# A new order of all steps in an attention and two-layer MoE kernel on one Trainium2 core

## The chip, the cores and the metric

The kernel runs on one core of a Trainium2 chip. The metric is device time in microseconds (us) of one execution. Five engines matter: TensorE (PE) with its weight loads (PEld), VectorE (DVE), ScalarE (ACT), GpSimd (POOL), and SyncE (SP), whose queue issues every DMA transfer here. Each engine works through its own queue strictly in the order in which the program issues; semaphores make it wait for others.

## The reference

For 4 batches and 8 heads, 768 time steps and head width 40, a gated linear attention with a stabilised state, then two feed-forward layers over 3072 tokens of width 320:

```python
for t in range(S):                                   # attention, per batch and head
    m_new = max(f[t] + m, i[t])
    C = exp(f[t] + m - m_new) * C + exp(i[t] - m_new) * outer(v[t], k[t])
    n = exp(f[t] + m - m_new) * n + exp(i[t] - m_new) * k[t]
    m = m_new
    y[t] = sigmoid(o[t]) * (C @ q[t]) / max(abs(n @ q[t]), 1)
h = x @ w_in                                         # layer 1: 320 -> 1024
solu = h * softmax(h)
x2 = ((solu - mean(solu)) / sqrt(var(solu) + 1e-6) * g_ln) @ w_out
h2 = max(x2 @ w1, x2 @ w2, x2 @ w3)                  # layer 2: 320 -> 768
out = h2 @ w2_out
```

## The kernel before, in words

The attention is done in chunks of 128 time steps: 24 tiles t, four batches of six chunks, all eight heads at once. A tile's 128 tokens then pass through layer 1, and each pair g of two tiles through layer 2. Products run in a 32-bit float form whose operands are split into a high and a low part (helper `split`, L274 and L276: ACT copies the high part, another engine subtracts it), so one product is two or three passes.

The program is a set of Python generators. Each does the work of one kind for one tile, pair or weight piece, and hands over at each `yield`; what stands between two yields is a step. The string `ORDER` names one step after another, and that is the order in which all instructions are issued, and so each engine's queue. In it `A0*2` is two steps of process A0, and a number behind `~` puts as many small products that nothing reads in front of the step's own, to keep PE active. The order is written out as it stands; nothing is chosen at run time.

```python
        for token in ORDER.split():
            token, _, z = token.partition("~")
            spare[0] = int(z or 0)
            name, _, n = token.partition("*")
            for _ in range(int(n or 1)):
                next(procs[name])
```

The processes, and what their steps issue:

- G: gates. Scans on DVE make the row maxima and decays; they are turned by PE, and rows_m, rows_g and rows_d go to DRAM to be read back spread over partitions.
- L*key*: loads of weight pieces, 640 KB each, 20 in all: in0 and in1 (two each), out0 to out3, nine m*, last0 to last2. D0 to D19 decode them (L249 to L299): two steps of ACT, two of DVE, an addition on GpSimd (L261), then the split or the scaling of the weights.
- Q*t*: loads q and k. From tile 6 on they are split (L274, L276), both parts go to DRAM (qks, L348) and come back stacked three times over 120 partitions as kst and qst (L355, six transfers of 160 KB), which have one buffer each. W*t*: the decay mask Wm, a 512 KB load (L385), a mask on GpSimd (L367), exponentials on ACT (L396). V*t*: values and keys. I*t*: gb, a 192 KB load of decays, and either its product with q (qg, L441, tiles under 6) or products pi of PE (L452). T*t*: the state (L464 to L492). S*t*.0 and S*t*.1: score products ps (L423) and their masking Pr (L426).
- Y*t*: output products py (L501 and on), copies, then a store of the denominators nd (L516) and of y (L517), three small DVE operations on nd (L519 to L521) and a store of rn (L523). X*t*: loads xr (L536 to L538) and nq (L540, spread from rn), products with the output gate and nq (L542, L544), and the split into xh and xl. O*k*: the output gate's sigmoid on ACT.
- A*t*: layer 1. Two products ph (L566), maxima (L569), exponentials (L573), u (L578), squares (L581), the scaling of u (L591), its transposes pu (L599), splits, the product px (L615), the transposes pq (L627) and the split of x2.
- U*g*: nine products pe of a pair (L650), in two PSUM buffers. P*g*: their maximum (ACT copies the first of three, L662; DVE takes the other two, L664) and its split. F*g*: products po with the output weights (L681), a copy and the store.

All transfers stand in one queue, SP's, so one that waits for its data holds back all that are issued behind it.

Of the kernel before, what the change touches and what calls it, by code (L numbers as in the profile page):

```python
# [63 lines left out]
Q12*2 A7 A9 W11*2 S11.0 A8 V11 U3 P2*3 F2 S11.1 A8 W12 A8*3 Q12 A8 W13*2 Y10 X10 Q13 I11*2 A8*2 A9 Y10*2 A8 Q12 T12
X10*2 T12*2 Y11 V13*2 A9*2 F2*3 W13 A9*2 X10*3 P3 Q13*2 F2 A9*2 U3 Y11 I11*2 P3 A10 A8 A10 T13*3 A8 T14 A9 Q12 A8 W12
A9 Y11 U3 P3*2 U3 A8 T13 S12.0 S12.1*2 A9 I13 Y11 P3*2 U3*2 Q14 A9 Q13 X11 Y11 S12.0 Y11 A9 T13*3 P3 A9*3 X11*2 A9*2
P3*3 Y12 A10*3 A9*3 Y12 Q13 Q14 U3 P3 U3 Y12 Q14 W14 U3 O4 A10 X11*3 Y12 I13 V14*2 W14 P3 Q14 P3 W13 I13 S13.0 S13.1*2
I13 U4*2 S13.0 O4 Y12 W14 X12 Q15 A10 Q15 Y12 A10*3 Q14 X12 W15 T14 Y13*2 T14*2 I13 Y13 A11 T15 A10*5 Q15 I14 W14
T14*3 A10 A11 Y13 A11 A10 X12*2 P3*2 A11*2 X12 W15*2 F3*3 A11*3 V15 S14.1 F3*2 Q15 S14.1 Y13*2 P4 X12 A12 I14*2 X13
V15 T15 S14.0 T15 Q16 A11*2 S14.0 I14*2 U4 T15*3 P4 A10 A11 A10 P4 T15 A11*4 P4 I15 P4 U4 P4 Y14*2 F3 Q16 Y14 A10  # L70
A12*2 A10 Q15 U4*2 V16 P4*2 X13 S15.0*2 A11*3 X13*4 W16 T16 V16 I15 S15.1 P4 A12 W15 A11 I15*3 A11 A12 P4 Q16*2 A11 U4
P4 U4 T16 A12*3 S15.1 P4 U4 P4 A13 W16*2 A12*5 Y14*2 A12 T16 A12 W17 Q17 X14 W17 P4*2 Y14 A12 X14 Y15 X14 A13*2 T16
F4*2 W17 F4 A12 X14 Y15*2 U5 Y15 U5 F4 A13 T16 W17 A13 X14*2 Q16 A13 Q17 I16 A14 P5 A13 Q17 A13 Y15 A12 S16.0 P5 S16.0
U5 P5 U5 W16 S16.1*2 P5 T16*2 I16*2 A13 P5 I16 A13 Q17 I16 Y15 A14 F4 Y16 A13*2 F2 U5 W18 A13*2 Q17 Q18 A12 Y16 V17
Y16 A12*2 A13*2 P5 A13*2 U5 A13 P5 A14*2 S17.1 P5 S17.0 V18 O5 A13 S17.0 P5 I17*2 U5 O5 A14 P5*2 X15*2 W18 A13 U5
A14*2 X15 P5 F4 X15 Y16 S17.1 Q18*2 X15*2 U5 P5*2 Y17 Y16 V18 W19 T18*2 A14 T18*2 Y16 I17*2 T18 I17 V19 U6 A15 I19 U6
W18 A14*4 W18 A15 Q18 A14*3 Y17*2 T19 A14 X16*2 Q19 Q18 Y17 A14*2 V19 P5 A15*3 F5*2 X16*2 F5*2 P6*2 W19 S18.0*2 A15
W19 A15*3 S18.1*2 T18 W20*2 A15 Q19*3 W19 A14*2 X17 F5*2 U6 T19*3 Y18 T20 Y18 P6 U6 A15*3 U6 Q19 A15*4 W20 P6*2 X16
Y18 W20 Y17 X16 A16*2 V20 A16 Y17 P6 X17*2 A14 U6 P6 A15 P6 V20 A16 S19.0*2 X17*3 A16 A15 I19 Q20 S19.1 P6 A15*2 P6
U6*2 Y18 P6*2 A16*2 T20 T19 S19.1 T20 A17 X18 O6 A17 Q20*3 U6 I19*2 A16 W21 A16*2 Y18 P6 A16*2 Y19 A16*2 T19*2 U7 A16  # L80
T20 Y18 X18 P6*2 I19 T20*3 A16*2 Y19*2 O6 X18 A17 Q21 A17 U7 Q21 Q20 A17 X18 F6 X18*2 A16 F6 V21 I20 T21 A18 S20.0 A18
Y19 X19 F6*2 Y19 S20.0 Y19 X19 A17*3 V21 A18 I20 F6 T21 P7 X19 P7 I20*2 W21 A16*2 T21 A17 T21 A16 U7*2 A17 S20.1 T22
P7 W21*2 P7 A17*2 U7 S20.1 Y20 Q21 A17*3 I20 P7 A17 Q21 P7*2 A17 U7 Q21 Q22 A17*3 X19 Y20*3 P7*2 U7 Y20 W22 A17 U7 Q22
# [5 lines left out]
X22*2 S23.0 A20 S23.0 Y23*2 U9 A21*2 X22*3 Y23 X22 Y23 F8*2 A21*4 A20 F8 A22*2 A21*4 F8 Y23*2 A21*3 X23*3 A20*2 P9 A22
P9 A21 U9 P9 U9 P9*3 A21 U9*2 A20 P9 A22*4 X23*2 A21 P9 X23 P9 F8 P9 U9 P9 U9*2 A22*3 P9*3 A21*2 A22*4 P9 A23*2 A22*4  # L90
A23*2 F9*3 A23*6 U10 F8 F9*2 A23 P10 A23*2 A22*2 U10*2 A23*5 P10 A22 U10 P10*3 A23 P10 U10 P10 U10 P10*2 U10 P10*2 F9
U10 P10 U10 A23*2 U11 P10*3 F10*4 P11 U11 U11~5 P11*4 U11*2 P11*2 U11*2 P11*4 U11*2 P11*4 F11*2 F10*2 F11*6
"""


# [700 lines left out]
```

## Time and profile before

| what | value |
|---|---|
| median of 3 runs | 656.64 us (656.39 to 660.28) |
| the profiled execution | 652.64 us |
| its span, first to last instruction | 650.8 us |
| mean granted clock of PE | 0.949 |
| PE busy | 602.9 us |
| DVE busy | 413.5 us |
| ACT busy | 329.8 us |
| GpSimd (POOL) busy | 211.2 us |
| DMA | 95.99 MB, mean 147 GB/s |

Busy is the time in which an engine has an instruction in work. A wait is idle time of an engine, put down to the instruction or transfer that ended it. The chain of waits is followed back from the last instruction, at each step to what released it. The clock is the share of 2.4 GHz that was granted; 0.5 is the other level, 1.2 GHz.

### The profile page before, as it was taken

Reading aid. Unit: us, or ns where it says so; the run is one execution under the profiler, and the core shown is the slowest. Engines: PE = TensorE matmul, PEld = TensorE weight load, DVE = VectorE, ACT = ScalarE, POOL = GpSimd, SP = SyncE. Lnnn points to the kernel's source line nnn. Section 1 sums busy time; section 2 is a strip of 40 time slices with the busy share of each in tenths; the row PEclk is TensorE's granted clock in tenths of the full one; section 3 lists DMA queues with packets and bytes.
Section 4 is the critical chain, followed back from the end, with each engine's and each line's share of the span. In section 5 each row is a group of like instructions: output and inputs, shape, how many; then the busy total and the mean of one; then the engine's idle time right before and its main releaser. Section 6 shows DMA issues by size and latency. Waiting matters only on the chain.

```text
span 650.8 us, 12480 instructions
## 1 busy us (share of the span) xinstructions
PE 602.9 (93%) x4688; PEld 550.0 (85%) x4688; DVE 413.5 (64%) x790; ACT 329.8 (51%) x693; POOL 211.2 (32%) x201
## 2 busy tenths in 40 slices
...
GB/s 302 292 237 297 106 199 129 122 114 110 132 177 172 186 223 163 121 184 220 165 203 138 112 176 159 193 180 164 139 123 187 130 170 51 46 1 32 2 11 31
DMA packets 56843, 95.99 MB, mean 147 GB/s; under 512 B 13926, under 2 KB 36510, under 8 KB 56782
## 3 DMA queue, kind: packets, MB, share of 16 engines
...
## 4 chain that ended last, share of the span: by engine, by line
PE 54%; DMA 21%; DVE 11%; ACT 5%; SPq 4%; issue 3%; POOL 2%; ACTq 0%; DVEq 0%; POOLq 0%
PE pe L650 20%; PE px L615 9%; PE ph L566 8%; PE po L681 7%; DMA Wm<-rows_m 3%; PE pu L599 3%; DMA rn<-nd 2%; PE py L501 2%; DMA gb<-rows_g 2%; DMA qst<-qks 2%; PE ps L423 2%; DMA ys<-y 1%; DMA nd<-y 1%; DMA qkr<-qt 1%; SPq L355 1%
## 5 line engine op out<-in xcount | busy, mean ns | idle before, releaser
L650 PE MATMUL pe<-x2h,w 128*128 128x256 f32 x1080 | 167.0, 285 | 4.6 <-ACT tmp L662 4.2
L650 PEld LDWEIGHTS pe<-x2h,w 128*128 128x128 f32 x1080 | 143.8, 188 | 7.3 <-ACT tmp L662 4.9
L650 PE MATMUL pe<-x2l,w 128*128 128x256 f32 x648 | 112.2, 282 | 0.0
L650 PEld LDWEIGHTS pe<-x2l,w 128*128 128x128 f32 x648 | 92.1, 188 | 0.0
L276 POOL TENSOR_TENSOR h<-tmp,h 128x512 fp32r<-128x512 f32 x33 | 44.2, 1339 | 138.8 <-ACT h L274 137.5
L664 DVE TENSOR_TENSOR tmp<-pe,tmp 128x512 f32<-128x512 f32 x72 | 49.4, 686 | 61.1 <-PE pe L650 52.0
L566 PE MATMUL ph<-w,xh 128*128 128x512 f32 x240 | 69.1, 420 | 7.0 <-ACT xh L274 6.5
L681 PE MATMUL po<-w,h 128*128 128x320 f32 x432 | 67.2, 310 | 0.0
L615 PE MATMUL px<-w,uh 128*128 128x320 f32 x384 | 66.9, 317 | 0.1
L681 PEld LDWEIGHTS po<-w,h 128*128 128x128 f32 x432 | 63.9, 188 | 0.4 <-issue 0.2
L396 ACT ACTIVATE Wm<-Wm,aT 128x128 f32<-128x128 f32 x184 | 58.1, 394 | 8.2 <-POOL Wm L367 8.1
L615 PEld LDWEIGHTS px<-w,uh 128*128 128x128 f32 x384 | 59.4, 193 | 1.6 <-ACT uh L274 0.9
L566 PEld LDWEIGHTS ph<-w,xh 128*128 128x128 f32 x240 | 45.3, 200 | 17.1 <-ACT xh L274 7.4
L274 ACT CAST h<-tmp 128x512 fp32r<-128x512 f32 x36 | 22.3, 621 | 58.9 <-DVE tmp L664 58.8
L274 ACT CAST uh<-pu 128x512 fp32r<-128x512 f32 x48 | 26.8, 588 | 46.4 <-PE pu L599 46.1
L367 POOL TENSOR_SCALAR_AFFINE_SELECT Wm<-Wm 128x1024 f32<-128x1024 f32 x24 | 26.4, 1101 | 65.1 <-DMA Wm<-rows_m 59.9
L276 DVE TENSOR_TENSOR ul<-pu,uh 128x512 fp32r<-128x512 f32 x48 | 32.3, 686 | 22.6 <-ACT uh L274 20.3
L578 DVE SCALAR_TENSOR_TENSOR u<-ph,e 128x1024 f32<-128x1024 f32 x24 | 29.2, 1217 | 26.9 <-ACT e L573 22.5
L426 DVE TENSOR_TENSOR Pr<-ps,Wm 128x512 f32<-128x512 f32 x48 | 32.1, 683 | 21.2 <-PE ps L423 20.5
L566 PE MATMUL ph<-w,xl 128*128 128x512 f32 x144 | 43.0, 408 | 0.7 <-DVE xl L276 0.6
L261 POOL TENSOR_TENSOR stA<-stA,raw 128x640 int32<-128x640 int32 x20 | 34.5, 1729 | 27.3 <-DVE raw L257 20.1
L573 ACT ACTIVATE e<-ph,st 128x1024 f32<-128x1024 f32 x24 | 26.9, 1121 | 25.2 <-PE px L615 14.7
...
## 6 DMA issues: line engine op xcount, KB each, us to landing
...
raw<-w SPq DMA_DIRECT2D x9, 640.0 KB
...
raw<-w_out SPq DMA_DIRECT2D x7, 640.0 KB
```

The costliest lines, as they stand in the source:

```text
L261: pt(out=i32(A), in0=i32(A), in1=i32(low), op=ALU.add)
L274: nc.scalar.copy(out=hi, in_=x)
L276: sub(out=lo, in0=x, in1=f(hi), op=ALU.subtract)
L396: nc.scalar.activation(out=W[:, h], in_=W[:, h], func=AF.Exp, scale=-1.0, bias=aT[:, c, b * H + h:b * H + h + 1])
L426: tt(out=Pr, in0=ps, in1=at[t, "W"][:, hh * 4:hh * 4 + 4], op=ALU.mult)
L566: mm(out_n, lhsT=a, rhs=x, start=(i == 0), stop=(i == len(passes) - 1))
L573: nc.scalar.activation(out=e, in_=ph, func=AF.Exp, bias=s(0), accum_out=s(2))
L578: nc.vector.scalar_tensor_tensor(out=u, in0=ph, scalar=-2.0 ** -15, in1=e, op0=ALU.mult, op1=ALU.mult, accum_out=s(3))
L615: mm(px, lhsT=a, rhs=x, start=(i == 0), stop=(i == len(passes) - 1))
L650: mm(pe[:, j], lhsT=a, rhs=x, start=(i == 0), stop=(i == len(passes) - 1))
L664: tt(out=tmp, in0=pe, in1=tmp, op=ALU.max)
L681: mm(po[o], lhsT=h2[:, a, m, o * P:o * P + P], rhs=made[f"last{m // 2}"][:, 0, x * WC + m % 2 * DM:][:, 0:DM], start=(m0 == 0 and i == 0), ...
```

## The change

`ORDER` is replaced as a whole. The new one has the same 1912 steps in another order, with the same numbers of extra products at the same steps. Nothing else is changed: the steps' bodies, their engines, the buffers and the transfers stay. Shown are the first twelve lines of both, to the first pe products and beyond, and the lines of later stretches that the text speaks of.

```diff
 ORDER = """
-G*2 Lin0 V1 G~14 G Lin0 G*3 W0 D0 W0*3 Q0 D1*3 Lin1*2 G D0*2 Lm0_0 O0 G V0 G*2 W0*2 G G~52 G*3 S0.1 D1*2 D2 B D0*2
-S0.0~5 D2 S0.0 Lout1 S0.1 G W1 Lout0 D2 V0 D2 T0~8 G D1 Q1 I1 D3 D1*3 W1*2 D3*4 D2 Y0 W2 S1.1 Lm0_1 I1 D1*4 D5*2 Lm2_1
-W1 Y0*2 S1.1 V1 S1.0~7 S1.0 T0 Y1 D4 W2 Y0 G T1 Y0 D4*3 Lout2 O0 B Lout3 D3*4 D4 D3*3 X0 Y1 Y0 X0 D3 D6 V2 Y1 W3 D7 V2
-T1*2 D5 X0 W2*2 V3 Y1 Q2 Llast2 I2 D7 X0*2 D6 Y1 Lm2_0 Lm1_0 X0 W3*2 A0~10 A0 S2.0 T2 D4 Lm1_1 Y1 D7 W3 D4 D7 D6*4 I2
-X1 Lm0_2 S2.1*2 S2.0 Llast1 T2 X1*2 Y2~9 Q3 D8*2 X1 A0*2 D5 A0 D5 Y2 A0*2 T2 T3 W5 D6 Y2 A0*2 X1*2 D8 A1~20 D8 V3 Y2
-I3*2 S3.1 A0 V4 Y2 S3.0 S3.1 D9 A0*3 Y2 D9 S3.0 A0 D5 A0 D7*2 W4 Q4 D9 W5 D7 T3 D5 D10*2 X2 A0 X2 T3 A1*2 Y3*4 W4*2 Y3
-D8 S4.0 W4 D8 D10 X2*3 D9*2 A0 A1 V4 A0 S4.0 A1 X2 Lm2_2 D9 W5 T4 S4.1 Y3 D8*2 D9*2 T4 O1 Q6 I4 S4.1 O1 A1*3 A2~2 A2
-X3*2 I4 Y4 D11*2 V6 Y4 Lm1_2 X3*2 A1 X3 D9 D8 A1*2 Y4 A1 Y4 Q5 D10 W6 D10 T4 A1*4 W5 D11*3 A1 A2*3 A0 S5.1*2 S5.0*2 X3
-D12 W6 I5*2 D12*4 A1*2 A0*2 A2*3 D11 D13 D11 X4 A2 D10*4 V5 Y5 D14*2 W7 A1 Y5 V7 A2*2 Y5*2 Llast0 D14 D12 V6 Y4 T6*2
-D12*2 A1 A2*2 Y4 A2 X4*2 Y5 Q6*3 D13 D12 D13*2 Q6 D11 A3*2 Q7 D11 D14 U0 A2 T6 A2*2 U0 D13 A3 T6 D17*2 T6 D15*2 X4*2
-A3 Y5 D15*2 X4 A3 P0 W6 D13 U0 P0*2 X5*2 A4*2 U0 D15*2 A3*3 T7 D13*3 D17 S6.0 D17 D14 D16*4 A2 Q7 P0*3 S6.0 W6 D14 D17
-D14*3 I7 A3*2 D18 U0*2 S6.1*2 A3 W7 D17*2 T6 D15 P0 V7 P0 A3*3 D19 A3 D19 D16 D15*2 A2 A3*3 A4 X5 A3 A2 P0 D18*2 X5 Q7
...
-Y7 A6 Y7 W9*2 T9 A6 T9 T10 A5*2 P1*2 Q8 A6 S8.0 A5 X7 S8.1*2 U1 S8.0 Y8 Y7 X7 I8*3 X7 I8 A5*2 Y8 Q9 X7 A6 Q9 U1 P1 I9
-X7*2 V10 U1 P1*4 W10 A7 Y8 Q10 A5 S9.1 Y8 S9.0 W10 I9 W9 I9*3 F0 A6 W10 U2*2 S9.0 V10 T10 S9.1 I10 Y8*2 Q10*3 Y9 A6*3
...
-W23*2 Q23 P8 Q23 P8*2 A19*2 U8 Y21 W23*2 X21 A19 P8 U8 A19*2 P8*3 A20 A19 S22.1 Y22 A20 P8 A20 Q23 A20 Q23 X21*3 U8
-A19 S23.1 Y22 P8 I23 U8 T22*3 X21 A20*2 S23.1 Y22 A21 P8*2 I23 A21 A20*4 P8 I23 A20 Y22 A21 Y22 U9 Y22 I23*2 V23 A20*2
...
+G*2 G~14 G*2 Lin0*2 G V0 G Lin1 W0*2 D1*2 Lin1 D0*2 O0 G*2 Q0 V1 W0 G*2 W0 Lout1 G G~52 D0 D2 D3 Lm0_0 G*2 W0 G S0.0~5
+S0.1 D1 G*2 W0 D0*2 D3 D1 W1 Q1 D2 S0.0 S0.1 Y0 Lout0 D1*4 B V1 G D2 V0 I1 D1 W1 Y0 D3 Y0 T0~8 D1 D2 D1*2 S1.0~7 D1 O0
+W1 D3*2 T0 S1.0 T1*2 Y0 D4 W1 T1 W2 S1.1 D8 S1.1 I1 Y1 Lout3 D2 D3*2 D4 X0 Y0 Lout2 D4 D3 Y0 D3 W3 D3 D4 D5*3 Y1*2 I2
+Y1 D3*3 D7*2 V2 D4 W2 B D4 X0*3 W3 Y1 D4 X0 X1 X0 A0~10 D6 D7 D8 D6 Q2 V2 S2.1 Llast1 S2.0 Y1 W2 X1*2 Lm0_1 D6*3 A0 W2
+S2.0 I2 S2.1 Y2~9 A0 D7 Lm1_0 T2 V3 Q3 D6 W5 D5 A0*4 D5 X1 T2 Lm2_0 T2 Y2*2 D8 A0 Y2 T3 S3.1 W3 D8 V3 A0 X1 D6 X1 A0
+I3*2 D7 A1~20 Y2 D5 D9 W3 X2 S3.1 S3.0*2 A1*2 W5 A0*3 Y3 D9*2 W5 D7 Lm0_2 Y2 T3 D5 A0*2 W4 Y3 X2 Q4 Y3 V4 A0 W4*2
+D10*2 D7 A0 D8*2 S4.1 Y3 Lm2_1 X2*2 Y3 D9 A1*2 W4 D9 X2 S4.0*2 D9 T3 V4 Lm1_1 D12 X2 A2~2 T4 S4.1 D8 A1*3 D9 I4 X3 I4
+D9*2 D11 O1 A1*2 T4*2 A2 D8*2 Y3 X3 A2 O1 D10 D12 Y4 A0 W7 W5 X3 D10 A1*2 X3 Q6 Q5 A1*4 V5 A1 D11*2 X3 Llast2 I5 D14
+D12 S5.1 D10 D11 D10 D12 A2 D11 D14 Y4 A2*3 S5.1 A0*3 Lm2_2 A2 D10 S5.0 Lm1_2 S5.0 D11 Y4*2 A1*4 I5 D10*2 Y4 Y5 D12
+Q6*2 D13 A2 V6 A2 D14 D12 X3 D11 A2*2 A3 D12*3 V6 U0 A3 X4 Y4 Q7 D13*2 Q6 Llast0 Y5*2 D15 D11 D13 D14 D15 Q7 A2*4 Y5
+X4 T6 P0 A2 U0 D11 D15 U0 D17*2 D15 X4 D13 D15 T6*2 A3 T7 W6 Y5*2 X4*2 D17 X4 A2 A3 P0 A3*2 T6 A3 P0 A3 D13*4 Q6 D16
+D17 T6 I7 D16*2 A4 W6 A2 A4 D14*3 S6.1 D16 P0*2 S6.0 A3 W6 D14 S6.0 D14 D17 D19 X5*3 D15 A3 X5 W6 S6.1 U0 P0 U0 A3*3
...
+S7.0 A4 S7.0 Q9 P1 Q9*2 U1 S7.1 Y7 A5 X6 A4 X6*2 P1*2 U1*2 P1 X6 V9 W9 A5*2 A6 Y7*2 A5*5 W9 P1*2 U1 I8 Y7 A5*3 W9 Y7
+A5*2 A4 T8 W8 P1 W8 A6*2 V9 A4*2 A5*2 Q8 W9 A6 S8.0 S8.1*2 P1 Y7 I8*3 Q10 I8 S8.0 U1 X7*5 T9 P1 A6 Y8 A5*2 X7 P1 T9 A6
+Q9 U1 A6 U1 Y8*2 I9*2 V10 P1*2 S9.0*2 T10 S9.1*2 V10 A6 W10*2 Y8 A7 W10 P1 I9*3 F0 A5 A6 Y8 Q10 Y8 Y9 A6 U2 A7 Y9*2 A6
...
+A7*3 P2*2 I10 U2 I10 P2 U2 P2 A8 X9*3 Y10 T12*2 X9 A8 P2 W11 U2 T10 Y10*2 P2 T13 P2 W11 Q11 S11.0 U2*2 I11 S11.0 A8*2
...
+A12*2 A11 A12 Y15 A13*2 Y15*3 W16 W17 U4 P4*3 U5 V18 F4*3 A12*2 Q17 A12*2 Q17 Y15 T16 F4 W17 A12 T16 A13 T16 X14 P5
...
+Q17 S16.1 A13 U5 P5 S16.1 I16*2 Q17 Y16*3 A13 A14 P5*2 U5*2 X15 A14 S17.1 A13*2 W18*2 A12*2 A13*5 P5*2 T16 U5 V18 Y16
...
+A14*4 Y15 X15*3 Q18 Y16 P5*2 I17 X15 F5 X15 W19*2 T19 A14*2 A15*2 A14 Q19*2 F5 T18 Q19 A14*2 X16*2 W18 A15 Q18 S18.0
...
+Q23 A18*2 Y20 F7 U8 F7 W22 I22 X20 A18 X20 A19*2 W22 X20*2 Y21 A19 X20*2 Q23*2 O7 U8 A18*2 P8 A20 A19*5 W23 U8 A19*2
+Y21 X21 Y21 Q23 I22 F7 Y21 X21 O7 X21 P8 T22 I22 U8 P8*2 U8 S22.0 P8 F6 P8 A19 S22.0 A19*2 T22 U8 P8 S22.1 I22*2 A19*2
+W23 A20 P8*3 S22.1 X21 Y22 W23 U8*2 A19 A20*3 X21 A20*2 T22 X21 A21 A20 Y22 A20 Q23 T22 S23.1 Y22 A19 T22 P8*2 T22 A20
...
 """
```

## Rows read from the trace of the kernel before

**Rows 1.** The page's first part: busy us, share of the span, instructions.
```profile
PE 602.9 (93%) x4688; PEld 550.0 (85%) x4688; DVE 413.5 (64%) x790; ACT 329.8 (51%) x693; POOL 211.2 (32%) x201
```

**Rows 2.** Busy time by stretch (us from start): length, engines, PEclk, DMA share, GB/s.
```profile
0.00:67.70 67.70, 50.61 (x355) 37.30 (x356) 52.14 (x96) 42.90 (x82) 31.10 (x28) 0.76 0.84 280
67.70:148.00 80.30, 68.99 (x456) 55.61 (x454) 67.82 (x117) 55.54 (x113) 45.12 (x37) 0.80 0.48 129
...
165.00:560.00 395.00, 380.96 (x3082) 357.53 (x3082) 250.82 (x502) 196.71 (x426) 107.65 (x111) 1.00 0.54 159
560.00:651.00 91.00, 87.67 (x668) 85.98 (x667) 28.29 (x55) 25.56 (x54) 14.28 (x13) 0.99 0.06 19
```

**Rows 3.** Waits of DVE, 0 to 165 us: total us, times, longest.
```profile
DVE nd L519 <- DMA nd<-y: 5.3, 2, 3.6
DVE stA L254 <- ACT stA L251: 4.7, 3, 2.1
DVE Pr L426 <- PE ps L423: 3.9, 2, 2.3
...
DVE xr L544 <- DMA V<-vn: 2.5, 1, 2.5
```

**Rows 4.** Waits of PE, 165 us to the end.
```profile
PE ps L423 <- DMA qst<-qks: 4.8, 3, 2.3
PE pe L650 <- ACT tmp L662: 2.9, 2, 2.2
PE ps L423 <- DMA nd<-y: 1.5, 1, 1.5
PE pi L452 <- DMA qst<-qks: 1.4, 1, 1.4
PE ps L423 <- DMA qks<-qkl: 1.1, 1, 1.1
...
PE ph L566 <- ACT xh L274: 0.2, 1, 0.2
```

**Rows 5.** The chain that ended last, 0 to 165 us: start us, us, what.
```profile
35.56 3.54 DMA rn<-nd
...
42.31 4.81 DMA nd<-y
...
48.27 9.63 DMA rn<-nd
57.99 4.04 DMA nq<-rn
...
64.33 1.39 DVE xl L276
```

**Rows 6.** The DMA queue (SP) in order of time, 44 to 59 us.
```profile
46.52 1.51 SPq L240 DMA_DIRECT2D raw<-w  x3
48.27 0.68 SPq L523 DMA_DIRECT2D rn<-nd  x1
```

**Rows 7.** DMA issues by source (20 pieces: 9, 7 of w_out, 4 of w_in).
```profile
raw<-w SPq DMA_DIRECT2D x9, 640.0 KB
```

**Rows 8.** The chain, whole span: PE steps at the full clock.
```profile
427.60 0.88 PE py L501 x16
...
472.15 2.64 PE po L681 x18
...
542.58 1.82 PE ph L566 x8
...
594.65 1.90 PE pe L650 x16
```

**Rows 9.** Timeline of DVE and of GpSimd (POOL), 64 to 76 us.
```profile
68.43 3.84 DVE L519 SCALAR_TENSOR_TENSOR nd<-nd 128x8 f32<-128x8 f32 x1
...
70.68 1.55 POOL L261 TENSOR_TENSOR stA<-stA,raw 128x640 int32<-128x640 int32 x1
```

**Rows 10.** Waits of the DMA queue (SP), whole span.
```profile
SPq L540 <- DMA rn<-nd: 36.2, 13, 4.9
```

More of the change, by code (lines that the diff above doesn't have):

```diff
@@ L64 @@
[L64 to L83, printed above, removed]
@@ L84 @@
-V22 P7*2 U7 X19*2 P7 F6 W22 T21*2 A18*3 Q22 I21*2 P7*2 S21.1 A19 S21.0*2 P7 I21 F7*2 Y20 S21.1 A18 A19 I21 A18*3 Q22*2
-A18*2 Y21 A18 I21 A18*2 V22 T22*2 X20 A19 X20*2 A18*3 A19 W22 Y21 F7 A19 I22 X20*2 T21 Y21 O7 Y21 X21 A19 X20 F7*3
-A19*2 U8*2 P8 I22*2 U8 P8 A18 P8 S22.0*2 I22*2 A20*2 A18 T22 A18 O7 A19*2 Y21 A20 S22.1 A19 W22 A19*2 Q23 U8*2 A19
-W23*2 Q23 P8 Q23 P8*2 A19*2 U8 Y21 W23*2 X21 A19 P8 U8 A19*2 P8*3 A20 A19 S22.1 Y22 A20 P8 A20 Q23 A20 Q23 X21*3 U8
-A19 S23.1 Y22 P8 I23 U8 T22*3 X21 A20*2 S23.1 Y22 A21 P8*2 I23 A21 A20*4 P8 I23 A20 Y22 A21 Y22 U9 Y22 I23*2 V23 A20*2
@@ L89 @@
[L89 to L92, printed above, removed]
+G*2 G~14 G*2 Lin0*2 G V0 G Lin1 W0*2 D1*2 Lin1 D0*2 O0 G*2 Q0 V1 W0 G*2 W0 Lout1 G G~52 D0 D2 D3 Lm0_0 G*2 W0 G S0.0~5
@@ new lines @@
+D17 T6 I7 D16*2 A4 W6 A2 A4 D14*3 S6.1 D16 P0*2 S6.0 A3 W6 D14 S6.0 D14 D17 D19 X5*3 D15 A3 X5 W6 S6.1 U0 P0 U0 A3*3
+U0 A2*2 D15 A3 D15*2 D17 Y6*2 P0*2 V7 A3 Y6 A3*2 A4 U0 D18 D16 D18 V7 D18 Q7 D17 P0 T7 A4 A3 D16*2 D18 D19 A3 A4 D16
+Q7 D16 P0*2 Q8 T7 A3 D18 U0*2 A3 P0*2 T6 V8 W7 Y6 A4*2 Q7 U1 X5 W7 X5 W8 U1 D19*3 A4 A5*2 X6 Y6*2 D18*2 D19 Q8 A4 I7
+A4 P0 O2 T7 P0 T7 D19 F0 I7 F0*2 Q8*2 A4 V8 T8*2 T7*2 T8 A4 Q9 A4 T9 A4*2 O2 A4 X6 F0*2 W8 I7*2 T8 A5 T8*2 P1 W7 S7.1
+S7.0 A4 S7.0 Q9 P1 Q9*2 U1 S7.1 Y7 A5 X6 A4 X6*2 P1*2 U1*2 P1 X6 V9 W9 A5*2 A6 Y7*2 A5*5 W9 P1*2 U1 I8 Y7 A5*3 W9 Y7
@@ new lines @@
+A5*2 A4 T8 W8 P1 W8 A6*2 V9 A4*2 A5*2 Q8 W9 A6 S8.0 S8.1*2 P1 Y7 I8*3 Q10 I8 S8.0 U1 X7*5 T9 P1 A6 Y8 A5*2 X7 P1 T9 A6
+Q9 U1 A6 U1 Y8*2 I9*2 V10 P1*2 S9.0*2 T10 S9.1*2 V10 A6 W10*2 Y8 A7 W10 P1 I9*3 F0 A5 A6 Y8 Q10 Y8 Y9 A6 U2 A7 Y9*2 A6
+X8 Q10*2 X8 T10 T9 A6 V12 T9*2 A6 W10 A6 T10 A6*3 Q10 P1 Q11 A7*5 T9 X8 U2 A7 X8*2 F1*3 T10*2 I10 F1 P2*2 A6*2 F1 Y9*2
+S10.1 A7*2 S10.1 U2*2 I10 S10.0 W11 X8 A8 S10.0 Q11*2 A7*3 P2 I10 P2 A7*2 A6 V12 O3 A8 O3 A8 T10 Q11 Y9 W12 A6 W12 X9
+A7*3 P2*2 I10 U2 I10 P2 U2 P2 A8 X9*3 Y10 T12*2 X9 A8 P2 W11 U2 T10 Y10*2 P2 T13 P2 W11 Q11 S11.0 U2*2 I11 S11.0 A8*2
```

31 lines of the change are left out of this document (25 added, 6 removed).

## The prediction

> **What bounds the kernel now.** The busy shares come first. TensorE (PE) is busy 93% of a span of 650.8 us [rows 1]; the profiled execution took 652.64 us, so 1.8 us lie around the span. The share hides two regimes, which the table of stretches parts [rows 2]. It is cut where two VectorE (DVE) steps start, A0's scaling of u (67.70 us) and A3's (148.00), both of L591. From 165 us on, PE is busy 380.96 + 87.67 = 468.6 of 486 us at the full clock, so it waits 17.4 us there. Up to 148 us it is starved: DVE is busy 52.14 of 67.7 us and 67.82 of 80.3 us, PE's mean granted clock is 0.76 and 0.80, and transfers run at 280 GB/s at first. The end can only come earlier if the head gets shorter or the 17.4 us do.
>
> What stops the two bounding engines is told by the waits. DVE idles 15.6 + 12.5 = 28.1 us up to 148 us. Up to 165 us, transfers end 5.3 + 2.5 = 7.8 us of its waits in the two largest groups of theirs, ScalarE (ACT) 4.7 and PE 3.9 in theirs [rows 3]. After 165 us PE waits for transfers 4.8 + 1.5 + 1.4 + 1.1 = 8.8 of its 17.4 us, and 2.9 for ACT's copy of a product [rows 4].
>
> The chain of waits shows why transfers cost so much early. To get a tile into the first MoE layer, three small round trips follow each other: y to nd, nd to rn, rn to nq. For tile 1 they took 4.81, 9.63 and 4.04 us; tile 0's rn, 4 KB too, took 3.54 [rows 5]. The DMA queue gives the reason: from 46.52 us it issued three weight pieces, and rn came right behind at 48.27 [rows 6].
>
> **The change part by part.** Every step stands in the new order as often as in the old (1912 in each) and has the same body, so work, bytes and engines stay. Only the queue order of each engine changes, SP's transfers among them. Three terms follow.
>
> *Weight pieces moved behind the first tiles (SP's queue).* Ahead of A0's first ph product the old order issues 14 of the 20 pieces of 640 KB [rows 7], the new one 9. Five pieces are 3.28 MB, at 280 GB/s 11.7 us of transfer. Between tile 1's nd and rn the old order has four pieces (last2, m2_0, m1_0, m1_1), the new one only last1. Three pieces less are 1.97 MB, 7.0 us at 280 GB/s; the two rn rows differ by 9.63 - 3.54 = 6.1, which I take.
>
> That is what the transfer saves, not the end, for DVE works in order: the same DVE steps (60 with it) lead up to A0's scaling of u in both orders, and to A3's the same plus one. So only DVE's idle time can go. Transfers end 7.8 us of it: at the nd of tiles 1 and 3 and at the first xr product. Now tile 1's nd is issued ahead of the first nq, so it has landed when DVE comes to it; five decoding and splitting steps stand between A1's maxima and tile 3's nd, where none stood. Against that, the first nq is issued behind W3's 512 KB, a gb and Y1's stores. I take two thirds, 5 us. Bounds: -2 (each wait finds a new place, and nq is late by the 2.5 us of the xr wait once more) and 11.7 (the whole volume counts).
>
> A page weighs this less. The Trainium skill's "DMA: Bandwidth & Descriptors", section "Anatomy of one DMA — SWDGE (gpsimd) path", gives about 2.0 us plus bytes over 436 GB/s, fitted on GpSimd's path. As an estimate by that page, three pieces less are 4.5 us, and the term would be 3.7 instead of 5. The trace's 280 GB/s [rows 2] disagrees, and decides.
>
> *The reload of q and k before a score product (SP's queue, PE's path).* From tile 6 on the split halves go to DRAM (qks) and come back stacked (qst, kst); S needs them. For tile 9 the old order has two pe steps and one ph product between qks and S: 2 x 1.90 + 1.82 = 5.6 us of PE work [rows 8]. S waited 2.3 us there, the longest qst wait [rows 4]. The new order has 21 PE steps between. But the reload also waits until tile 8's pi products free the single buffer; behind those, the new order has a pe and a py product more and the ph less, 1.90 + 0.88 - 1.82 = 1.0 us [rows 8], so this wait shrinks by 1 only. Tile 23's single pe step becomes 14 PE steps. Tiles 11 and 17 get tighter: some 7 us of PE work stand behind the freed buffer, about a us more than at tile 9 before. I take 4 of the 8.8 us; bounds 8.8 (all go) and -4.6 (nothing goes, and tiles 11 and 17 each wait tile 9's 2.3).
>
> *What pays for it.* Hand-overs between engines get shorter: more often the first pe product of a pair directly follows the second tile's split, and pair 4's output product starts one pe step behind the pair's last. ACT's copies already cost PE 2.9 us [rows 4]. I take -1; bounds 0 and -2.9, twice as many.
>
> Nothing else has a term: the eight sigmoids each still stand between exponentials on ACT, the warm-up products keep their steps, and after U11 PE's last products follow as before.
>
> The sum is 5 + 4 - 1 = 8 us: 652.6 becomes 644.6 on the profiled execution. The median of the three runs, 656.64, lies 4.0 above that execution; with the same 8 us it becomes **648.6**.
>
> **The rivals.** *DVE's busy time grows by what its idle time loses (no change).* Busy time holds blocked time: tile 2's nd, 8 elements a row, took 3.84 us and ended at 72.27, when GpSimd's add begun at 70.68 did [rows 9]. If shorter waits bring two more DVE steps beside such work, 2 x 3.84 = 7.7 us go: 0.3 is left, 656.3. For it: in the new order too tile 2's nd stands right behind A0's scaling, with gb's product and that add in a row on GpSimd. Against it: most DVE steps keep their neighbours. The Trainium skill's "SBUF — State Buffer", section "SBUF: two separate sides", says that the port pair shared by these two is an exclusive lock for a whole instruction, so the loser is blocked, not slowed; the trace agrees with its 3.84 us.
>
> *Transfers are the whole brake (much faster).* The head gains the 11.7 us of volume, the 8.8 us of PE's waits go, and 1 is paid: 19.5, so 637.1. For it: rn's 9.63 us. Against it: ACT and PE end as much of DVE's waiting as transfers [rows 3].
>
> *SP loses its lead (slower).* One queue issues every transfer. In the new order tile 15's rn has one po product, 2.64 us [rows 8], between it and A15's first ph, and tile 20's nq one pe product, 1.90. From nq's issue to the end of the split tile 1 took 64.33 + 1.39 - 57.99 = 7.7 us, and rn's 3.54 come ahead [rows 5]. If SP, DVE and GpSimd run no further ahead of PE than the text of the order, A15 waits 3.54 + 7.7 - 2.64 = 8.6 us and A20 5.8, together 14.4. With the second term gone, 14.4 + 1 - 5 = 10.4: 667.0. It decides once those waits pass 4 us, the head's 5 less 1. For it: SP already stands 36.2 us waiting for rn [rows 10]. Against it: the old order leaves A7 4.6 us of PE work behind its rn, and after 165 us all ph waits for xh sum to 0.2 [rows 4].
>
> That the executed order is another can be left out: each engine runs its queue as issued.
>
> **How the numbers follow.** A measurement of this kernel can tell about 1%, 6.6 us, from no change. The forecast has 0.49, its own range 643 to 653, some seven tenths of it under 650.1. No change has 0.27, much faster 0.13, slower 0.11. Faster by over 1%: 0.7 x 0.49 + 0.13 = 0.47. Slower by over 1%: 0.10, a little of that rival staying inside. Within 1%: the rest, 0.43. The range is 638 to 661: below it lies half of the much faster case, above it most of the slower one.
>
> **What would show it.** Right: DVE's waits for transfers up to 165 us near 3 us; A3's scaling of u near 143 instead of 148; tile 1's rn near 3.5 us; PE's waits for transfers after 165 us near 5. Wrong: A3's scaling at 148 again (the head is DVE's); new ph waits for xh at A15 or A20; pe waits for ACT's copy well over 2.9.

## The result and the profile after

The changed kernel takes 630.8 us (median of four runs, 629.4 to 632.6) against 656.5: a ratio of 0.9611, 95% interval [0.9549, 0.9672], 25.7 us less. The forecast was 8 us less, 648.6, with a range of 638 to 661. The direction is right; the time lies under the range. Measured once more beside the experiments, on another chip, the ratio was 0.9624 [0.9580, 0.9668], 24.7 us (run after_again below). The sizes of the experiments are taken against that second ratio.

The profiled execution took 632.62 us with a span of 630.8, 20.0 us less than the profiled one of before: 8.1 us are won by the end of pair 0's ninth pe product (163.6 us before, 155.5 after), 11.9 behind it. First the busy line of after (us, share, instructions), then the busy time by stretch at the cuts used before (length; PE, PEld, DVE, ACT, POOL; PEclk, DMA share, GB/s; the last stretch is shorter as the span is).

```profile
PE 595.1 (94%) x4688; PEld 546.3 (87%) x4688; DVE 399.4 (63%) x790; ACT 329.7 (52%) x693; POOL 214.4 (34%) x201
```

```profile
0.00:67.70 67.70, 51.71 (x362) 38.09 (x363) 53.61 (x101) 43.43 (x84) 35.27 (x30) 0.80 0.77 245
67.70:148.00 80.30, 69.20 (x495) 55.87 (x495) 67.60 (x122) 59.04 (x120) 50.55 (x41) 0.89 0.55 162
165.00:560.00 395.00, 390.19 (x3185) 370.59 (x3185) 245.13 (x509) 198.96 (x432) 106.79 (x112) 1.00 0.52 157
560.00:631.00 71.00, 67.73 (x521) 66.60 (x519) 18.37 (x32) 17.30 (x35) 10.71 (x10) 1.00 0.04 15
```

Against [rows 1, 2]: from 165 us on PE is busy 390.19 + 67.73 = 457.9 of 466 us, so it waits 8.1 us where it waited 17.4. In the head PE was granted 0.80 and 0.89 of its clock instead of 0.76 and 0.80. DVE's busy time fell by 14.1 us; it did not grow.

The waits of after, DVE's from 0 to 165 us (the largest group, and the largest that a transfer ends), and PE's four largest from 165 us on:

```profile
DVE Pr L429 <- PE ps L426: 5.8, 3, 4.2
...
DVE gi L180 <- DMA gi<-ig: 0.2, 1, 0.2
```

```profile
PE ps L426 <- DMA xr<-ys: 2.0, 1, 2.0
PE ph L569 <- DVE xl L279: 1.0, 1, 1.0
PE pc L475 <- POOL kw L418: 0.8, 1, 0.8
PE pi L455 <- DMA qst<-qks: 0.8, 1, 0.8
```

The transfers that ended 7.8 us of DVE's idle time [rows 3] are gone. At PE 2.0 + 0.8 = 2.8 us of transfer waits are left of 8.8 [rows 4], and the 2.9 us for ACT's copy are gone as well. A score product ps reads only qst and kst: where another transfer is named beside it, as xr here, that is the one whose end the profile matched to its start. In a second execution of this kernel (after_again) the same wait stands under qst.

The view that tells most is the chain between 300 us and the last attention tiles. First before (300 to 500 us), then after (300 to 480 us): shares of the stretch by engine and line, then its longest pieces (start us, us, what).

```profile
by line: PE pe L650 13.7%; PE ph L566 7.6%; DMA qst<-qks 6.3%; PE px L615 5.7%; issue 5.4%; DMA qkr<-qt 4.2%; DMA qkr<-kt 3.5%; DMA kst<-qks 3.4%; DMA xr<-ys 3.4%; DMA ys<-y 3.3%; DMA Wm<-rows_m 3.1%; SPq L355 3.0%; DMA qks<-qkl 3.0%; PE po
...
385.13 8.41 DMA qkr<-qt
```

```profile
by line: PE pe L653 27.9%; PE ph L569 14.4%; PE px L618 12.4%; PE po L684 8.9%; DMA kst<-qks 3.4%; DMA qst<-qks 3.2%; PE ps L426 3.1%; PE pu L602 3.0%; PE py L504 2.2%; DMA qks<-qkl 1.9%; issue 1.6%; PE pi L455 1.4%; PE pq L630 1.3%; DMA xr
...
392.04 6.20 DMA kst<-qks
409.14 5.83 DMA qst<-qks
```

Adding up the pieces by kind, 70.9 us of the old chain's 200 are transfers and 19.4 more SP's issuing, and only 75.3 are PE. After, it is 17.5 and 6.1 of 180, with 135.3 on PE. In the old body PE was busy 95% of that stretch (189.6 of 200 us), and still the chain ran beside it, on a path through transfers that was nearly as long. The links of a chain are inferred; one of them does not hold (below, at U5's ninth product).

### The profile page after: what moved, and what is told of

Its sections match the earlier page's. It is cut to its first block, busy times and chain, and to the rows that moved or that the text cites. A ratio compares the mean times of both kernels' runs of the same rounds, so it can differ in the third digit from the quotient of the medians.

```text
span 630.8 us, 12481 instructions
## 1 busy us (share of the span) xinstructions
PE 595.1 (94%) x4688; PEld 546.3 (87%) x4688; DVE 399.4 (63%) x790; ACT 329.7 (52%) x693; POOL 214.4 (34%) x201
## 4 chain that ended last, share of the span: by engine, by line
PE 53%; DMA 4%; SPq 2%; DVE 1%; ACT 1%; issue 1%; POOL 0%; ACTq 0%; DVEq 0%; POOLq 0%
PE pe L653 23%; PE ph L569 8%; PE px L618 8%; PE po L684 7%; PE pu L602 2%; PE py L504 2%; PE ps L426 1%; DMA kst<-qks 1%; DMA qst<-qks 1%; DMA kw<-kn 1%; PE pq L630 1%; PE pi L455 1%; DMA qks<-qkl 1%; SPq L358 0%; PE pc L475 0%
## 5 line engine op out<-in xcount | busy, mean ns | idle before, releaser
L667 DVE TENSOR_TENSOR tmp<-pe,tmp 128x512 f32<-128x512 f32 x72 | 49.4, 686 | 47.9 <-PE pe L653 38.3
L569 PE MATMUL ph<-w,xh 128*128 128x512 f32 x240 | 67.4, 412 | 5.6 <-ACT xh L277 5.5
L569 PEld LDWEIGHTS ph<-w,xh 128*128 128x128 f32 x240 | 43.5, 194 | 14.2 <-ACT xh L277 5.9
L592 POOL TENSOR_TENSOR st<-st,nhalf 128x1 f32<-128x1 f32 x24 | 16.9, 703 | 84.7 <-DVE st L590 72.9
L569 PE MATMUL ph<-w,xl 128*128 128x512 f32 x144 | 41.6, 397 | 1.4 <-DVE xl L279 1.4
```

Of the source, the lines that this page charges most:

```text
L569: mm(out_n, lhsT=a, rhs=x, start=(i == 0), stop=(i == len(passes) - 1))
L667: tt(out=tmp, in0=pe, in1=tmp, op=ALU.max)
```

## Experiments

Sizes are ratios to before, measured on the same chip, times that chip's median of before. Two kernels' sizes are compared through their ratios. "PE loss" in the expectations is PE's elapsed time less its steps' own time at the full clock. Each order keeps every process's own sequence of steps.

### The head alone, the body alone

Two orders spliced at the end of pair 0's ninth pe product (163.6 us before): h_after is new, then old; h_before is old, then new.

```diff
 ORDER = """
-(old order up to U0's ninth step) (old order)
+(new order up to U0's ninth step) (what is left, in the old order)      h_after
+(old order up to U0's ninth step) (what is left, in the new order)      h_before
 """
```

> The new order up to pair 0's ninth pe product (U0, 163.6 us before, 155.5 after), then the steps that are left in the old order's sequence. The two traces put 8 of the 20 us between the profiled executions ahead of this point. Theory 1 (head and body are two gains that add): a lead won in the head is kept to the end, since PE is almost never idle behind it: 8 us less than before, about 648.5. Theory 2 (the body takes it back: transfers or DVE limit the body in the old sequence, so an earlier start only means longer waits): 0 to 4 us less, 652.5 to 656.5. The recorded forecast sized this part at 5 us: 651.5.

Measured 0.9947 [0.9913, 0.9980]: 3.5 us less (1.3 to 5.7). That is within theory 2 and short of theory 1's 8 us. The lead itself is there: A3's scaling of u starts at 141.8 us in this trace and at 140.3 to 141.8 in all six traces with the new head, against 148.0 to 151.9 in the ten with the old one. Why the old body does not keep it is open; the profiled execution, 645.6 us and the fastest of ten, did keep 7.0 us of it against before's 652.6.

> The old order up to pair 0's ninth pe product, then the steps that are left in the new order's sequence. Theory 1 (two gains that add): 12 us less than before, about 644.5, and PE idle after 165 us near the 8 us of the changed kernel instead of 17. Theory 2 (the body's gain needs the new head, for example because weight pieces that are still to be decoded fill the body differently): under 6 us less, above 650.5. The recorded forecast sized this part at 4 - (-1), that is 3 us net: 653.5.

Measured 0.9789 [0.9712, 0.9866] with four runs, so it was taken again.

> The old head with the new body once more, as four executions between 636.6 and 645.5 us left the ratio 0.9789 with a wide interval (0.971 to 0.987). If head and body add up to the changed kernel's 0.962, this is 0.962 + 1 - 0.995 = 0.967. If the new body is worth only 0.979 behind the old head, some 8 us need both.

Measured 0.9767 [0.9728, 0.9806]: 15.2 us less, interval 12.7 to 17.8. This is the largest part of the gain, and the forecast had 3 us for it. PE's busy time in this profile:

```profile
165.00:560.00 395.00, 391.34 (x3177) 370.94 (x3178) 251.02 (x515) 200.09 (x436) 109.68 (x115) 1.00 0.54 161
```

PE waits 3.7 us there instead of 14.0 [rows 2]. The two parts sum to 18.7 us; 24.7 came again with the changed kernel itself. The 6.0 us between are more than the uncertainty of the three ratios together (some 4.4 us), so the sum falls short: some of the gain seems to need both parts. How much, and by what, stays open.

> The changed kernel itself, for a ratio on the same chip as the others. The first measurement gave 0.9611. If the two gains add as h_after (0.9947) and h_before (0.9789) have it, 0.974 is expected; if 0.961 comes again, some 8 us arise only when the new head and the new body stand together.

Measured 0.9624 [0.9580, 0.9668], not the 0.974 of two gains that add.

### Weight loads alone

w_later is the old order with loads of weight pieces moved back to about where the new one has them: last1 alone stands between tile 1's nd and rn, and with it ten pieces, not nine, ahead of A0's first product. w_earlier is the reverse in the new order.

```diff
-... Lm0_1 ... Lm2_1 ... Y1 ... Llast2 ... Y1 ... Lm2_0 Lm1_0 ... A0~10 ... Lm1_1 Y1 ... X1 Lm0_2 ... Llast1 ... X1
+... Y1 ... Y1 Llast1 ... A0~10 ... Y1 ... X1 ... X1 Lm0_1 ... Lm0_2 ... Lm1_0 ... Lm1_1 ... Lm2_0 ... Lm2_1 ... Llast2
```

> The old order with nothing but loads of weight pieces moved: nine pieces instead of fourteen stand ahead of A0's first product, and one (last1) instead of four between tile 1's nd and rn, as in the new order; every other step keeps its place. The recorded forecast, whose first term is exactly this: 5 us less, 651.5, tile 1's rn near 3.5 us instead of 9.6. Rival, the whole volume counts: 11.7 us less, 645. Rival, the head is held by DVE's own work and by hand-overs, the weights are hidden anyway: 0 to 2 us less, 654.5 to 656.5, with rn short all the same.

Measured 0.9951 [0.9905, 0.9997]: 3.2 us less (0.2 to 6.2).

> The new order with nothing but loads of weight pieces moved back: fourteen instead of nine ahead of A0's first product, four between tile 1's nd and rn, as in the old order. Forecast's term: 5 us more than the changed kernel, 636, with tile 1's rn near 9.6 us again. If the weights are all of the head's gain: 8 us more, 639. If the weights are hidden and the head's gain is in the sequence of the other steps: 0 to 2 us more, 631 to 633.

Measured 0.9697 [0.9626, 0.9769]: 4.8 us more than the changed kernel, with some 5.5 us of uncertainty on the difference. Both agree with the forecast's 5 us and neither reaches the 11.7 of the whole volume, but w_earlier cannot be told from no loss at all. SP's queue in w_later shows the shorter round trip at tile 1 (start us, us, what), and DVE's waits from 0 to 70 us where the time went instead; last, tile 2's nd:

```profile
49.98 0.34 SPq L523 DMA_DIRECT2D rn<-nd  x1
...
53.85 0.54 SPq L540 DMA_DIRECT2D nq<-rn  x1
```

```profile
DVE Pr L426 <- PE ps L423: 4.6, 2, 3.1
...
DVE nd L519 <- DMA nd<-y: 3.6, 1, 3.6
```

```profile
68.99 0.16 DVE L519 SCALAR_TENSOR_TENSOR nd<-nd 128x8 f32<-128x8 f32 x1
```

From rn to nq 3.9 us pass instead of the 9.7 of [rows 5], but DVE now waits 3.6 us for nd in this stretch (1.8 before, in the same stretch) and longer for a score product. A0's scaling of u starts at 68.3 us, no earlier than in the ten traces with the old head (67.3 to 71.0); only A3's is earlier, at 145.8 instead of 148.0 to 151.9. Tile 2's nd, 3.84 us in [rows 9], takes 0.16. In w_earlier A0's scaling is late, at 68.6 us (62.5 to 66.5 in the six traces with the new head), but A3's starts at 142.1, next to their 140.3 to 141.8. So most of the new head's lead at A3 stands without the pieces.

### PE's order repaired where it stalled

pe_local puts one or two PE steps (with the DVE step that feeds them) ahead of each of seven stalled steps of the old body; SP's queue is untouched. In this kernel T18's product stands ahead of the scaling of its keys, so that state is built from unscaled keys; the work is the same.

```diff
-... A5 S9.1 Y8 S9.0 ... U2*2 ...
+... A5 U2*2 S9.1 Y8 S9.0 ...
```

> The old order with seven local edits, SP's queue untouched: at S9, I13, S15, S16, S18 and S20 one or two PE steps that stood right behind the stalled product are put ahead of it (U2 twice; U4's first; A11's px; U5's third; U6's third; A18's second ph), and Y17's and T18's product ahead of U5's ninth. These seven stalls lost 12.6 us in the profile of before. Theory 2 (each is local, PE had other work ready): 8 to 11 us less, ratio 0.983 to 0.988, PE loss after 160 us from 29 to about 19 us. Theory 1 (SP is late as such): the stalls move to the next products that need q and k, 0 to 4 us less, 0.994 to 1.0.

Measured 0.9982 [0.9947, 1.0016]: nothing gained. PE's waits after 165 us, the two largest groups and what is left of the q and k reload and of ACT's copy, and then the chain ahead of the longest wait but one:

```profile
PE py L501 <- DVE Pr L426: 4.1, 2, 3.5
PE pc L472 <- POOL kw L415: 3.7, 2, 3.4
...
PE ps L423 <- DMA nd<-y: 0.7, 1, 0.7
PE pe L650 <- ACT tmp L662: 0.5, 1, 0.5
```

```profile
210.44 9.20 DMA Wm<-rows_m
...
219.71 1.09 POOL Wm L367
220.80 0.70 POOL kw L415
...
221.54 0.79 PE pc L472 x16
```

The transfer waits are gone as intended, and the same time is now waited for GpSimd and DVE. The chain says what for: a load of Wm that took 9.2 us, its mask on GpSimd, and kw in the queue behind the mask. At this place PE had not been late by itself; the stall only moved down the transfer path. By its size this is theory 1's result, though the stalls moved to products that need kw and Pr, not to the next ones that need q and k.

### One queue's order with the other engines' old one

sp_after gives SP's queue the new order behind 163 us and leaves the computing engines the old; cp_after is the counterpart. sp_free keeps all four computing queues and reorders SP's by a rule.

```diff
-SP old, PE, DVE, ACT and GpSimd old               before
+SP new, PE, DVE, ACT and GpSimd old               sp_after
+SP old, PE, DVE, ACT and GpSimd new               cp_after
+SP ready ones first, PE, DVE, ACT and GpSimd old  sp_free
```

> Up to pair 0's ninth pe product the old order. Behind it SP's queue takes its transfers in the new order, while PE, DVE, ACT and GpSimd keep the old one (33 transfers are pulled forward by up to 11 places, where a step of the old order needs them earlier). Theory 1 (the body's gain is SP's: q and k come back in time because SP is no longer held by loads of Wm whose buffer is not free, 27.8 us of waiting before, none after, and by nq behind rn): most of h_before's 14 us, ratio near 0.982, qst waits of PE after 165 us under 2 us. Theory 2 (the body's gain is in the order of the computing engines: hand-overs and the PE work that stands ahead of each score product): 0 to 3 us, ratio 0.995 to 1.0, the stalls at S9, S15, S16, S18 and S20 remain.

Measured 1.0862 [1.0806, 1.0918]: 57 us more.

> The counterpart: up to pair 0's ninth pe product the old order; behind it PE, DVE, ACT and GpSimd take their steps in the new order, SP keeps the old order of its transfers (31 pulled forward, most by under 7 places). Theory 1 (the gain is SP's): 0 to 4 us less, ratio 0.994 to 1.0. Theory 2 (the gain is the computing engines'): most of h_before's 14 us, ratio near 0.982, and no wait of pe for ACT's copy. If neither kernel alone gains more than a third, the two queues have to change together.

Measured 1.1488 [1.1436, 1.1539]: 98 us more.

> The old order in PE, DVE, ACT and GpSimd, every one of these queues as it was. Behind pair 0's ninth pe product SP's queue alone is put in another order: wherever the trace of before shows SP standing at a transfer that waits, the next one within 14 places whose data and buffer were ready goes first (188 of 225 steps change place, issued 4.9 us earlier on average by the old trace's times). Theory A: the old body loses its time to a held SP queue; 6 to 14 us less than before, ratio 0.979 to 0.991, few qst waits of PE after 165 us. Theory B (the order of the computing engines was the poorer part): 0 to 3 us, 0.995 to 1.0. Theory C (the transfers themselves are too many at a time: what goes ahead delays the rest): slower than before, above 1.0.

Measured 1.0225 [1.0185, 1.0264]: 15 us more. The theories of the first two runs had no loss in them. Each queue order is good only with the other that it was made with. The largest group but one of SP's waits in sp_after and the largest of PE's in cp_after, both behind 165 us:

```profile
SPq L347 <- ACT qkh L273: 36.1, 6, 8.7
```

```profile
PE ps L424 <- DMA qst<-qks: 20.2, 3, 8.4
```

In the first SP stands for copies that the old ACT order makes later; in the second PE stands for q and k that the old SP order brings later. So the question of the first two runs, SP's order or the engines', has no answer: the gain is neither's alone. sp_free shows that it does not help to let SP take whatever is ready, at least by this one rule: behind 165 us SP's waits at Wm fell from 27.8 to 10.8 us, but those for rn rose from 22.9 to 52.3 and those for ys from 13.3 to 47.9.

### One kind of transfer moved

wm_early and nq_early move one kind of load earlier in the new order; wm_late moves five loads of Wm back in the old one; wm_pool issues them from GpSimd's queue.

```diff
 wm_early, tile 19:
-S17.0*2 T16 A13 A14*2 ... X15 F5 X15 W19*2
+S17.0*2 W19 T16 A13 A14*2 ... X15 F5 X15 W19
 nq_early, tile 13:
-Y13 U4 X12 W16 ... T16 A12*2 P4*2 Q16 X13 T15 ... T15 X13 A12 X13
+Y13 X13*2 U4 X12 W16 ... T16 A12*2 P4*2 Q16 T15 ... T15 A12 X13
 wm_late, tile 18:
-U5 W18 A13*2 Q17 Q18 A12 Y16 V17 ... S17.0 V18 O5 A13
+U5 A13*2 Q17 Q18 A12 Y16 V17 ... S17.0 V18 O5 W18 A13
 wm_pool:
-            dma(out=W, in_=rows_m[c, bh].unsqueeze(0).to_broadcast([P, H, P]))
+            (nc.gpsimd.dma_start if t >= 8 else dma)(out=W, in_=rows_m[c, bh].unsqueeze(0).to_broadcast([P, H, P]))
```

> The new order with one kind of transfer moved: from tile 8 on the load of Wm stands as early in SP's queue as it may, right behind the second Pr of the tile two back, whose end frees its buffer (up to 15 transfers earlier, 92 places over 16 tiles). In the old order 7 of these loads were issued within 0.3 us of the Pr that freed the buffer, so SP stood waiting for it, 27.8 us in all; in the new one none. Theory A (what the body gained is that SP no longer stands still on buffers that are not free): SP waits for Pr 30 us or more again and the end comes 5 to 14 us later than the changed kernel, ratio to before 0.970 to 0.984. Theory B (SP's standing still is hidden, the gain lies elsewhere): within 2 us of the changed kernel, 0.959 to 0.966, or a little faster, as the masks are there earlier.

Measured 1.0221 [1.0172, 1.0269]: 39 us more than the changed kernel, more than theory A's bound. SP's group of waits for Pr behind 165 us and PE's largest group over the whole span:

```profile
SPq L387 <- DVE Pr L428: 63.8, 10, 9.3
```

```profile
PE pe L652 <- ACT tmp L664: 7.7, 4, 5.7
```

```profile
165.00:560.00 395.00, 368.32 (x2917) 346.73 (x2916) 230.91 (x467) 185.62 (x405) 103.54 (x107) 0.97 0.51 153
```

Not one wait of PE's names Wm. From 165 to 560 us PE waits 26.7 us instead of 4.8, and its mean granted clock is 0.97 instead of 1.00. The largest group, 7.7 us, is of pe products that wait for ACT's copy, the kind of wait that the forecast had put down to hand-overs.

> The new order with the loads xr and nq of 16 tiles from tile 6 on put directly behind the store of rn on which nq depends (25 transfers that stood between now come behind nq). In the old order 9 of 18 tiles had them adjacent and SP waited 22.9 us for rn after 165 us, in the new one 11.2. Theory A, with the price of wm_early (0.6 us per us of SP's waiting): about 20 us of waiting more, 8 to 12 us slower than the changed kernel, ratio 0.975 to 0.981. Rival (a wait of 3 us at rn is shorter than SP's lead and stays hidden, only long waits at Wm count): 0 to 3 us, 0.962 to 0.967.

Measured 0.9849 [0.9803, 0.9895]: 15 us more than the changed kernel for 25 transfers that now come behind an nq, again over the bound. SP's waits for rn behind 165 us rose from 11.2 to 24.7 us.

> The old order with five loads of Wm moved back (tiles 8, 12, 17, 18, 19: two to five transfers that stood behind each now go ahead of it); PE, DVE, ACT and GpSimd keep their orders. These five were issued within 0.1 us of the Pr that freed the buffer, so SP stood waiting there. Theory A (SP's standing still at a buffer that is not free is what the old body pays for): the reverse of wm_early, which lost 38 us to 64 us of such waiting, 0.6 us each; some 20 us of waiting less would be up to 12 us, and as nq, y and nd still hold SP, half of it: 4 to 8 us less, ratio 0.988 to 0.994, and the stall of U5's ninth product at 401 us gone. Theory B (what waits at one place waits at the next, as after the seven local edits): 0.997 to 1.003.

Measured 1.0060 [1.0024, 1.0096]: 4 us slower, though SP's waiting at Wm fell from 27.8 to 12.9 us.

> The old order unchanged; from tile 8 on the loads of Wm are issued from GpSimd's queue instead of SP's. GpSimd is the engine that masks Wm next, so it waits for that load anyway, and SP is never held by it. Theory A: SP's 27.8 us of waiting for Pr go, 4 to 12 us less, ratio 0.982 to 0.994. Theory B: no gain in the body, and GpSimd, which now stands waiting for Pr itself, delays kw, xr and the h2 parts: 0.998 to 1.02.

Measured 1.0029 [0.9994, 1.0063]: no gain. So the old order's waiting at Wm (SP's L385: 27.8 us behind 165 us) is not by itself what it paid for. Taking one kind of wait out of a poor order gains nothing, while putting the same kind into a good one costs at once.

### A stretch of the body

stretch_new is the old order with the new sequence between pair 3's and pair 7's ninth pe product, stretch_old the reverse.

```diff
+(old up to U3's ninth) (new up to U7's ninth) (what is left, old)      stretch_new
+(new up to U3's ninth) (old up to U7's ninth) (what is left, new)      stretch_old
```

> The counterpart: the new order, with that stretch in the old order's sequence, then what is left in the new one's. Theory A: the 11.5 us are lost again, ratio 0.962 + 0.0175 = 0.980. Theory B (the lead of the new order ahead of the stretch carries it through the old sequence): 0.962 to 0.970.

Measured 0.9760 [0.9725, 0.9795]: 8.9 us of the 24.7 lost again, near theory A. PE's waits in it from 300 to 500 us:

```profile
PE ps L425 <- DMA qst<-qks: 3.2, 2, 1.7
PE pe L652 <- ACT tmp L664: 2.0, 2, 1.4
PE ps L425 <- DMA Wm<-rows_m: 1.8, 1, 1.8
PE ps L425 <- DMA gb<-rows_g: 1.5, 1, 1.5
```

They stand at S15, S16, S18, S20 and at U5's and U7's ninth product, the very steps that stalled before, although everything ahead came in the new order. The stalls belong to the sequence of that stretch.

> The old order, with the steps between pair 3's and pair 7's ninth pe product (some 304 to 497 us) in the new order's sequence, then what is left in the old one's. PE's time beyond its products' own, counted by 20 us, was 18.4 us between 300 and 500 us in the profile of before and 6.9 in that of after, 11.5 of the 12.5 us that the body saves there. Theory A (the gain belongs to the stretch in which the rows show it): 9 to 13 us less than before, ratio 0.980 to 0.986. Theory B (it needs the order ahead of it, a lead of SP's that is built up earlier): 0 to 5 us, 0.992 to 1.0.

Measured 1.0055 [1.0024, 1.0087]: slower, against theory A. PE's waits from 300 to 520 us:

```profile
PE py L501 <- DVE Pr L426: 5.0, 2, 4.5
PE po L681 <- POOL h L276: 2.8, 1, 2.8
```

The first stands at 311 to 316 us, the second at 507 to 510 us: at the two seams, where one order expects work done that the other has not yet begun. Between the seams the old stalls are gone, as in after. So a stretch shows its gain only without the seams, and stretch_old has seams as well; if seams only cost, its 8.9 us are an upper bound of what the stretch is worth.

## Why the prediction was wrong

*Term H, the weight pieces (5 us): the size agrees, the reason given does not.* 3.2 us (0.2 to 6.2) in the old order, 4.8 (give or take 5.5) in the new. The rows moved in part further than forecast: DVE has no wait of note for a transfer up to 165 us (forecast near 3 us), and A3's scaling starts at 140.3 us (near 143). Tile 1's rn did not: from its store to nq 44.65 to 49.46, 4.8 us, not 3.5. But the term stood on "So only DVE's idle time can go", and that failed. Up to A3's scaling, in before, after and w_later (the third busy time is DVE's):

```profile
0.00:148.02 148.02, 119.62 (x809) 92.91 (x809) 119.96 (x213) 98.43 (x195) 76.24 (x65) 0.78 0.65 198
```

```profile
0.00:140.28 140.28, 114.05 (x796) 87.42 (x796) 115.18 (x214) 97.53 (x194) 81.11 (x65) 0.84 0.69 210
```

```profile
0.00:145.83 145.83, 115.44 (x809) 89.78 (x809) 115.58 (x212) 98.44 (x195) 76.49 (x65) 0.81 0.66 201
```

In after DVE's idle time is 3.0 us less (28.1 to 25.1), its busy time 4.8. In w_later the busy time is 4.4 less and the idle time 2.2 more. This is not one trace's chance: the ten with the old head have 26.9 to 32.3 us of idle time and 118.4 to 121.5 of busy time, the six with the new one 25.1 to 27.8 and 113.6 to 116.2. In w_later the waits found new places, and what went is blocked time, 3.7 us of it at tile 2's nd alone. That the sum came near 5 is in part luck. With the old body, the whole new head was worth 3.5 us.

*Terms B and C, the body (4 - 1 = 3 us): the step that failed; 15.2 us (12.7 to 17.8).* B said: "I take 4 of the 8.8 us; bounds 8.8 (all go)". That took for the price of transfers those waits of PE that a transfer ended last. C counted PE's 2.9 us for ACT's copy as hand-overs and expected them to grow. The queues of before contradict both. U5's ninth pe product waited 2.2 us for ACT's copy; here are SP's longest wait ahead of it, then SP's queue, ACT's and PE:

```profile
SPq L385 <- DVE Pr L426: 6.6, 1, 6.6
```

```profile
382.33 0.32 SPq L385 DMA_DIRECT2D Wm<-rows_m  x1
...
390.10 0.33 SPq L319 DMA_DIRECT2D sig<-og  x1
```

```profile
398.08 1.28 ACT L321 ACT_TABLE_LOAD   x1 [3.16 <-DMA sig<-og]
399.37 1.16 ACT L321 ACTIVATE sig<-sig 128x1152 f32<-128x1152 f32 x1
400.44 0.57 ACT L662 COPY tmp<-pe 128x512 f32<-128x512 f32 x1
...
402.88 0.51 ACT L274 CAST xh<-xr 128x384 fp32r<-128x384 f32 x1
```

```profile
401.06 0.85 PE L650 MATMUL pe<-x2h,w 128*128 128x256 f32 x5 [2.22 <-ACT tmp L662]
```

SP was held at Wm, 6.6 us, until a Pr freed its buffer at 382.3. Behind that stood the reloads of q and k and others, so sig, the output gate's load, was issued at 390.1. ACT waited 3.2 us for it, then did O5's sigmoid, and the copy came behind that. A wait that names ACT was a wait for transfers, on a path 19 us long. (The profile's chain leads from Wm over qkr and the loads of xr to the copy. That link does not hold: the split of that xr stands behind the copy in ACT's queue, at 402.9.) The prediction gave the sigmoids no term. Behind 165 us ACT waits 7.7 us for sig in before and 6.0 in h_after, both with the old body, and not at all in after and h_before2, with the new one; no run moves these loads alone.

Hence the bounds were too narrow: not 8.8 but all 17.4 us of PE's waiting were within reach, and 10.3 of the 14.0 up to 560 us went in h_before2. The other 4.9 us of its 15.2 are more than the interval covers (some 2.6 either way). One candidate is the clock after a wait. w_later, too, has the old body:

```profile
165.00:560.00 395.00, 382.95 (x3059) 360.55 (x3054) 245.07 (x498) 195.40 (x424) 108.46 (x111) 0.98 0.53 158
```

PE's mean granted clock is 0.98 here and 1.00 in before, and from A3's scaling to the end it took 507.0 us instead of 502.8, though PE waits 1.9 us less in this stretch. How often an execution of before goes this way is not on record, so the share of the clock stays open.

*The rivals.* "Transfers are the whole brake" came closest (637.1) and was given 0.13, too little for the same reason; its 637.1 is still 6 us long, as it too took 8.8 for the body. "DVE's busy time grows" is refuted, 413.5 to 399.4 us, but what it was about, blocked time, did move, the other way: tile 2's nd, 3.84 us in [rows 9], took 0.16, as GpSimd stood waiting for gb beside it:

```profile
63.19 0.16 DVE L522 SCALAR_TENSOR_TENSOR nd<-nd 128x8 f32<-128x8 f32 x1
```

"SP loses its lead" did not happen at A15 and A20: no wait of ph for xh is among PE's groups. As a mechanism it is the one to fear: wm_early and nq_early made SP lose its lead elsewhere and paid 39 and 15 us.

*What stays open.* No single part of the new order was found that carries the body's gain. The runs bound it: not seven repairs of PE's order (pe_local), not SP's order or the engines' alone (sp_after, cp_after), not the waits at Wm alone (wm_late, wm_pool). What is shown is that the old sequence of one stretch brings its stalls back behind the new order too (stretch_old), and that between 300 and 500 us the chain ran largely through transfers before and through PE after.
